# Lightning attention into a gated feed-forward layer: 64-token sub-blocks with two heads stacked on partitions, two sequences at once, crossbar transposes from block 8

## Chip, cores and metric

One core of one Trainium2 chip. Times are device microseconds (us) of one execution. A time is the median of a kernel's runs. Engine names are those of the profile: PE is TensorE's matmuls and PEld its weight loads, DVE is VectorE, ACT is ScalarE, POOL is GpSimd, SP is the sequencer that issues most DMAs here, and "SPq" and "POOLq" are the queues in which DMAs are issued.

## The reference, cut

```python
# q, k, v: (4, 8, 768, 64) float32;  lam: (8,);  w_in: (512, 2048);  w_out: (2048, 512)
for b in range(nb):                         # blocks of 64 tokens
    intra = (qb @ kb^T) * Dmask             # Dmask = lam ** (i - j) where i >= j, else 0
    out   = intra @ vb + (qb * lam_pow) @ kv_state
    kv_state = lam ** 64 * kv_state + (kb * rev_pow)^T @ vb
x = out as (3072, 512)                      # tokens x (heads * head_dim)
h = x @ w_in
out = (h * cos(h)) @ w_out                  # (3072, 512)
```

The feed-forward part is the larger one by far: 704 matmuls of 512 columns and 128 of 256 on PE. Attention feeds it.

## The kernel before: the parts that the change touches

A tile is 128 tokens of one sequence with all 8 heads, and there are 24 of them. The decay is split: q is scaled by a power of lam, v by its inverse. So the mask is of zeros and ones. A planner in the kernel simulates the engines and so fixes the order of instructions on every engine. What it decides is static program order: an instruction whose data is late holds up everything behind it on its engine.

```python
TILES = [4, 2, 4, 4, 4, 4, 2]                       # tiles per feed-forward group
ORDER = "b0 b1 b2 b3 i0 i1 i2 i3 o0 o1 o2 o3"       # first loads: tiles and weight chunks
...
# loads: one DMA of 256 KB per tensor and tile, 128 partitions (tokens)
i = nc.sync.dma_start(out=t, in_=src[b, :, s0:s0 + P, :].transpose([1, 0, 2]))
...
# transposes of q and k on PE, 8 matmuls of 128 columns per tile, then a DVE copy out of PSUM
nc.tensor.transpose(live["t", n][:, i, p, :], src[:, 2 * p:2 * p + 2, :], ident)
...
# q made block-diagonal (two heads per 128 partitions) by two DVE copies
nc.vector.tensor_copy(q_bd[n % NQ][h, :, i, :], t[h, 0, :, :])
...
# scores: 4 matmuls of 256 columns per tile
nc.tensor.matmul(t[:, 2 * i:2 * i + 2, :], lhsT=live["qkT", n][:, 1, p, :],
                 rhs=q_bd[n % NQ][:, p, :, :], start=True, stop=True)
...
# values: state and two heads, 12 matmuls of 128 columns per tile
nc.tensor.matmul(t[:, p, :], lhsT=kv_bd[(n - 1) % NK][:, p, :], rhs=live["qkT", n][:, 0, p, :], ...)
for i in range(2):
    nc.tensor.matmul(t[:, p, :], lhsT=v_pad[n % NV][:, 2 * p + i, :], rhs=live["s_m", n][:, 2 * p + i, :], ...)
```

## Time and profile before

| of the kernel before | value | view |
|---|---|---|
| time | 235.73 us (235.50 to 235.96, 2 runs) | run times |
| span | 233.6 us | the page |
| PE busy | 220.6 us, 94% | the page |
| first feed-forward matmul | 24.90 us | PE in order of time |
| DMA rate from 45 to 70 us | 228 GB/s | busy time by stretches |

The page is read from the top: busy time tells which engine is nearly full (PE), the rows of 40 slices tell when (a digit is the busy share of 5.84 us in tenths), and the chain of waits tells whether the full engine is also what sets the end. The lines are in the prediction below. One view that it does not show is that of PE's waits. Each line names the waiting engine and what ended the wait, then the us in total, how often, and the longest. In the kernel before no wait of PE on scores was longer than 1.1 us, and none of them was for a DMA:

```profile
PE ps_s L296 <- DVE qkT L271: 1.8, 3, 1.1
```

### The profile page before, as it was taken

How to read it: one execution, taken by the hardware profiler on the slowest of the kernel's cores; microseconds unless marked ns; L12 is line 12 of the kernel's file. 1: busy time of each engine (PE TensorE's matmuls, PEld its weight loads, DVE VectorE, ACT ScalarE, POOL GpSimd, SP SyncE). 2: the span in 40 equal slices, each digit the busy share in tenths (PEclk: the TensorE clock that was granted, in tenths of full speed). 3: DMA queues.
4: the chain of work that ended last, by engine and by line, in shares of the span. 5: the costliest groups of instructions: out<-in, count | busy, mean ns of one | idle time of the engine just before them, and what ended most of it. 6: DMA issues, size and time to landing. Idle time of an engine off the chain costs nothing.

```text
span 233.6 us, 4414 instructions
## 1 busy us (share of the span) xinstructions
PE 220.6 (94%) x1698; PEld 131.2 (56%) x1698; DVE 148.3 (63%) x279; ACT 106.6 (46%) x179; POOL 71.7 (31%) x108
## 2 busy tenths in 40 slices
PE   4887998899999999999999999999999999999993
PEld 4777543457776655555555555555555454556541
DVE  5577487087999998986685585685674563423210
ACT  5453676123445464554444445345345435544420
POOL 2569200486758665333314314412000000000000
PEclk9999999999999999999999999999999999999999
DMA  6997999999999999999562110110011011111112
GB/s 123 222 198 120 208 191 203 225 219 217 254 222 248 222 219 225 243 218 201 137 158 68 48 45 1 48 46 8 37 48 45 0 48 45 45 45 48 45 45 90
DMA packets 82868, 29.64 MB, mean 127 GB/s; under 512 B 75552, under 2 KB 79904, under 8 KB 82848
## 3 DMA queue, kind: packets, MB, share of 16 engines
q1 hardware_dynamic: 78480, 25.05, 48.6%
q0 software_dynamic: 4224, 4.19, 11.0%
q8 instruction: 13, 0.21, 0.4%
q10 hardware_dynamic: 144, 0.13, 0.2%
q14 instruction: 7, 0.06, 0.1%
HBM read 27.27 MB, written 6.29 MB: 144 GB/s over the span
## 4 chain that ended last, share of the span: by engine, by line
PE 71%; DVE 11%; DMA 10%; POOL 3%; ACT 2%; issue 1%; POOLq 0%
PE ps_f L410 30%; PE ps_h L372 26%; DMA w_out_sb<-in_moe_w_out_dram 8%; PE ps_s L296 4%; PE ps_t L266 4%; PE ps_o L341 4%; DVE q_bd L277 3%; DVE g L385 3%; DVE s_m L303 2%; DVE qkT L271 2%; PE ps_o L338 1%; PE ps_kv L316 1%; DMA lam_bc<-in_lam_dram 1%; POOL w_in_sb L214 1%; DVE kv_bd L325 1%; POOL w_out_sb L217 1%
## 5 line engine op out<-in xcount | busy, mean ns | idle before, releaser
L379 ACT ACTIVATE cos<-ps_h,halfpi 128x512 f32<-128x512 f32 (+1 forms) x107 | 66.3, 624 | 73.5 <-PE ps_h L372 73.4
L385 DVE TENSOR_TENSOR g<-ps_h,cos 128x512 bf16<-128x512 f32 (+1 forms) x107 | 64.5, 609 | 49.2 <-ACT cos L379 48.0
L410 PE MATMUL ps_f<-w_out_sb,g 128*128 128x512 bf16 x368 | 92.8, 379 | 1.4 <-ACT o_sb L423 0.7
L372 PE MATMUL ps_h<-xT,w_in_sb 128*128 128x512 bf16 (+1 forms) x428 | 93.7, 347 | 0.1
L372 PEld LDWEIGHTS <-w_in_sb 128*128 128x128 bf16 x448 | 43.0, 98 | 36.0 <-issue 0.4
L410 PEld LDWEIGHTS <-g 128*128 128x128 bf16 x384 | 35.9, 98 | 34.4 <-issue 2.2
L250 POOL TENSOR_TENSOR v_pad<-v_f,v_scale 128x256 bf16<-128x256 f32 x48 | 29.1, 626 | 46.7 <-PE ps_o L341 30.1
L303 DVE TENSOR_TENSOR s_m<-ps_s,mask 128x512 bf16<-128x512 f32 x48 | 31.3, 684 | 4.2 <-PE ps_s L296 4.1
L235 POOL TENSOR_TENSOR q_s<-q_f,q_scale 128x512 bf16<-128x512 f32 x23 | 24.0, 1043 | 22.5 <-PE ps_f L410 18.7
L271 DVE COPY qkT<-ps_t 128x1024 bf16<-128x1024 bf16 (+1 forms) x28 | 17.2, 614 | 17.3 <-PE ps_t L266 16.9
L423 ACT COPY o_sb<-ps_f 128x512 f32<-128x512 f32 x23 | 13.5, 586 | 21.7 <-PE ps_f L410 21.7
L277 DVE COPY q_bd<-qkT 64x512 bf16<-64x512 bf16 x48 | 19.6, 409 | 0.7
L341 PE MATMUL ps_o<-s_m,v_pad 128*128 128x128 bf16 x192 | 19.7, 221 | 0.4 <-DVE s_m L303 0.4
L350 ACT CAST xT<-ps_o 128x512 bf16<-128x512 f32 x24 | 14.0, 585 | 13.1 <-PE ps_o L341 13.0
L296 PE MATMUL ps_s<-q_bd,qkT 128*128 128x256 bf16 x96 | 15.6, 279 | 2.7 <-DVE qkT L271 1.8
L244 POOL CAST k_b<-k_f 128x512 bf16<-128x512 f32 x20 | 12.4, 620 | 17.6 <-issue 13.3
L341 PEld LDWEIGHTS <-v_pad 128*128 128x128 bf16 x192 | 14.9, 99 | 3.5 <-issue 0.5
L338 PE MATMUL ps_o<-qkT,kv_bd 128*128 128x128 bf16 x80 | 15.3, 219 | 0.0
L296 PEld LDWEIGHTS <-qkT 128*128 128x128 bf16 x96 | 8.8, 99 | 9.7 <-DVE q_bd L277 2.2
L325 DVE CAST kv_bd<-ps_kv 64x256 bf16<-64x256 f32 x32 | 13.4, 418 | 1.2 <-PE ps_kv L316 1.0
L468 PE MATMUL ps_h<-ident 128*128 128x64 bf16 x226 | 12.1, 211 | 1.6 <-POOL ident masks.py:199 1.6
L468 PEld LDWEIGHTS <-ident 128*128 128x128 bf16 x226 | 10.8, 111 | 1.8 <-POOL ident masks.py:199 1.6
(39 smaller groups left out, 93.1 us busy)
## 6 DMA issues: line engine op xcount, KB each, us to landing
q_f<-in_q_dram SPq DMA_DIRECT2D x24, 256.0 KB, 4.8
k_f<-in_k_dram SPq DMA_DIRECT2D x24, 256.0 KB, 4.8
v_f<-in_v_dram SPq DMA_DIRECT2D x24, 256.0 KB, 4.9
out_dram<-o_sb SPq DMA_DIRECT2D x23, 256.0 KB, 2.0
w_in_sb<-in_moe_w_in_dram POOLq DMA_DIRECT2D x4, 512.0 KB, 8.4
w_out_sb<-in_moe_w_out_dram POOLq DMA_DIRECT2D x4, 512.0 KB, 15.5
out_dram<-o_sb SPq DMA_DIRECT2D x1, 128.0 KB, 1.7
out_dram<-o_sb ACTq DMA_DIRECT2D x1, 128.0 KB, 1.7
```

Of the source, the lines that this page charges most:

```text
L235: eng.tensor_mul(t, live.pop(("q_f", n)), q_scale[:, c, :].unsqueeze(2).to_broadcast([P, H, D]))
L250: nc.gpsimd.tensor_mul(v_pad[n % NV][:, i::2, i * D:(i + 1) * D], src[:, i::2, :], v_scale[:, c, i::2].unsqueeze(2).to_broadcast([P, NP, D]))
L271: nc.vector.tensor_copy(live["qkT", n][:, sides], live["t", n][:, sides])
L277: nc.vector.tensor_copy(q_bd[n % NQ][h, :, i, :], t[h, 0, :, :])
L296: nc.tensor.matmul(t[:, 2 * i:2 * i + 2, :], lhsT=live["qkT", n][:, 1, p, :], rhs=q_bd[n % NQ][:, p, :, :], start=True, stop=True)
L303: nc.vector.tensor_mul(live["s_m", n][:, 4 * half:4 * half + 4, :], live.pop(("s", n, half)), mask.unsqueeze(1).to_broadcast([P, 4, P]))
L341: nc.tensor.matmul(t[:, p, :], lhsT=v_pad[n % NV][:, 2 * p + i, :], rhs=live["s_m", n][:, 2 * p + i, :], start=(i == 0 and c == 0), stop=( ...
L372: ins = nc.tensor.matmul(t[:, :cols], lhsT=w_in_sb[:, kd, f * P:(f + 1) * P], rhs=live["xT", i][:, kd, :cols], start=(kd == 0), stop=(kd = ...
L379: nc.scalar.activation(c[:, :cols], live["h", i, f][:, :cols], AF.Sin, bias=halfpi)
L385: nc.vector.tensor_mul(live["g", i][:, f, :cols], live.pop(("h", i, f))[:, :cols], live.pop(("c", i, f))[:, :cols])
L410: nc.tensor.matmul(live["f", i, j], lhsT=live["g", i][:, f, j * P:(j + 1) * P], rhs=w_out_sb[:, f, :], start=(f == 0), stop=(f == KF - 1))
L468: nc.tensor.matmul(idle_ps[:, :cols], lhsT=ident, rhs=ident[:, :cols], start=True, stop=True)
```

## The change

The intent is less work on PE. Blocks of 64 tokens halve the score and value columns, because less work above the diagonal is done. Two heads are stacked on the partitions: token t of head 0 on partitions 0 to 63, of head 1 on 64 to 127. So k and v (instead of q) are made block-diagonal. Two sequences are treated at once, as a pair of tiles; there are 12 pairs. From pair 4 (block 8) on, q and k are transposed by the DMA crossbar instead of PE. The diff, cut to its core:

```diff
-ORDER = "b0 b1 b2 b3 i0 i1 i2 i3 o0 o1 o2 o3"
+ORDER = "b0 b1 i0 i1 i2 i3 o0 o1 o2 o3"
+DMA_FROM = 4
...
-    for t in v_pad + q_bd + kv_bd:
-        nc.vector.memset(t, 0.0)
+    for a, b in zip(k_bd, v_bd):
+        nc.vector.memset(a, 0.0)
+        nc.gpsimd.memset(b, 0.0)
+    for a in kv_bd:
+        nc.gpsimd.memset(a, 0.0)
...
-                i = nc.sync.dma_start(out=t, in_=src[b, :, s0:s0 + P, :].transpose([1, 0, 2]))
+            x = x[b:b + 2, :, c * P + s * D:c * P + (s + 1) * D, :].rearrange("b (p i) s d -> i s (b p) d", i=2)
+            for h, i in halves:                       # partitions 0 to 63, then 64 to 127
+                ins = start(live[name, m][h, s], x[i])
...
+        def prep_vb(s):                               # v block-diagonal, on DVE
+            for h, i in halves:
+                nc.vector.tensor_copy(vb[h, s, :, :, h], live["v_c", m][h, s])
...
+        def transposes_dma(name, s):
+            nc.sync.dma_start_transpose(out=live[name, m][:, s].rearrange("t b p m -> t (b p) m"), in_=src)
...
+            if m >= DMA_FROM:
+                o, t = dma("SP", 1.2, 1.3, partial(transposes_dma, name, s), 2 * m - 6 + 0.1 * s + (name == "kT"),
+                           [ready], get=get, ordered=False)
...
-                    nc.tensor.matmul(t[:, 2 * i:2 * i + 2, :], lhsT=live["qkT", n][:, 1, p, :],
-                                     rhs=q_bd[n % NQ][:, p, :, :], start=True, stop=True)
+                    nc.tensor.matmul(t[:, s, p, :], lhsT=live["kT", m][:, s, x, p, :],
+                                     rhs=live["qT", m][:, 0, x, p, s * D:(s + 1) * D], start=True, stop=True)
```

## The prediction

> **What bounds the kernel now.** I read the page first: busy times, the slices and the chain of work that ended last.
>
> ```profile
> PE 220.6 (94%) x1698; PEld 131.2 (56%) x1698; DVE 148.3 (63%) x279; ACT 106.6 (46%) x179; POOL 71.7 (31%) x108
> ...
> PE   4887998899999999999999999999999999999993
> ...
> DMA  6997999999999999999562110110011011111112
> GB/s 123 222 198 120 208 191 203 225 219 217 254 222 248 222 219 225 243 218 201 137 158 68 48 45 1 48 46 8 37 48 45 0 48 45 45 45 48 45 45 90
> ...
> PE 71%; DVE 11%; DMA 10%; POOL 3%; ACT 2%; issue 1%; POOLq 0%
> ```
>
> PE (TensorE) is full from about 25 us to the end and carries 71% of the chain. The DMA row is as full as it gets, at 190 to 254 GB/s, from the start to about 105 us, and nearly empty after that. A slice is 5.84 us. So there are two regimes: a first half in which both PE and DMA are full, and a second half that is PE alone.
>
> Because a busy PE is not a PE at its peak, I next took the instructions in order of time, which give the rate of each kind of matmul once it runs back to back:
>
> ```profile
> 24.07 0.89 PE L468 MATMUL ps_h<-ident 128*128 128x64 bf16 x25
> 24.90 1.89 PE L372 MATMUL ps_h<-xT,w_in_sb 128*128 128x512 bf16 x8
> ...
> 51.00 0.39 PE L266 MATMUL ps_t<-ident,k_b 128*128 128x128 bf16 x4
> ...
> 62.37 0.60 PE L372 MATMUL ps_h<-xT,w_in_sb 128*128 128x256 bf16 x4
> ...
> 226.93 2.75 PE L410 MATMUL ps_s<-w_out_sb,g 128*128 128x512 bf16 x12
> ```
>
> The spans include some 0.2 us of pipeline depth (one lone matmul of 128 columns takes 0.22 us). Taken off, a 128-column matmul costs 56 ns, a 512-column one 216 ns, a 256-column one 109 ns, and a 64-column one 29 ns, its own weight load included. All are columns / 2400 + 2.5 ns. With these rates I counted PE's own instruction order from the first feed-forward matmul (24.90 us) on: 704 of 512 columns (152.0 us), 128 of 256 (14.0), and for the attention of the last 20 tiles 452 of 128 and 80 of 256 columns (33.9 us). Sum 199.9 us. The last matmul ends at 229.7, that is 204.8 us after the first, so only 4.9 us are lost in the whole steady part. A tail of 3.9 us follows (evacuation, store, end). The median of the times is 2.1 us above the profiled span.
>
> Last, the DMA queue's issues:
>
> ```profile
> 39.80 0.37 SPq L199 DMA_DIRECT2D q_f<-in_q_dram  x1
> ...
> 47.84 1.08 SPq L199 DMA_DIRECT2D v_f<-in_v_dram  x1
> 49.01 1.09 SPq L199 DMA_DIRECT2D q_f<-in_q_dram  x1
> ...
> 117.35 0.37 SPq L199 DMA_DIRECT2D q_f<-in_q_dram  x1
> ```
>
> An issue takes 0.37 us when the queue is free and about 1.08 us when it is full: 256 KB per 1.1 us is the transfer rate itself, so SP (the issuing sequencer) is held back by the transfers. The loads of tile 4 start only at 39.8 us, after the third w_out chunk has landed. From there to 105 us every load goes out as fast as the DMA engines take it.
>
> **What the Trainium skill says.** "TensorE: Matmul & The Clock Gate", Back-to-back issue gap: warm, N / 2.4 + 2.5 ns, with a floor of about 25 ns up to 64 columns; the trace agrees (29 ns at 64, 56 at 128, 216 at 512). "DMA: Bandwidth & Descriptors", Queues, rings and completion order: each engine takes descriptors in ring order; the trace agrees as far as the steady 4.8 us to landing behind a full queue goes. The same page, Latency and other measured facts, gives a crossbar transpose 261 GB/s; no run yet shows it, and I estimate 256 KB at 1.0 to 1.2 us. The same page, Rules for kernel authors, says transfers to the two partition halves serialize: the split k and v loads will not be faster than whole ones.
>
> **The change part by part, on PE.** Per tile before: 8 transposes (0.45), 4 score matmuls of 256 columns (0.44), 4 updates (0.22), 12 values (0.67), together 1.78 us. After, per pair of tiles: 16 scores, 16 updates, 32 values, all of 64 columns: 64 x 29.2 ns = 1.87 us, so 0.93 us per tile. Blocks of 64 tokens halve the score and value columns, because above-diagonal work is no longer done. Transposes are 24 per pair (k is block-diagonal, thus twice as many): 1.34 us per pair for pairs 0 to 3, and none on PE from pair 4. Counted in the changed instruction order from the first feed-forward matmul: 152.0 + 14.0 unchanged, 616 of 64 columns (18.0), 48 transposes (2.7): 186.6 us. The gain on PE is 199.9 - 186.6 = 13.3 us, 5.6% of the time.
>
> The other engines. DVE (VectorE) loses q_bd (two of 0.41 us per tile), one transpose evacuation of 0.69 per tile from pair 4 and half of the state copies, and gains the v_bd copies (four of 0.41 per pair): some 3.7 us per tile become 2.2. It was 98% busy from 60 to 80 us, so this stage gets easier. POOL: per pair 2.1 (q) + 2.5 (k in four pieces) + 2.1 (v) = 6.7 us against 2 x 2.9 = 5.8 before, well under the 15.5 us that PE needs per pair. ACT gains two state copies of 0.37 to 0.6 per pair, off the path. At the start POOL gets six memsets and both q products; the start is bound by loads of the same size, so I leave it at 24.9 us, give or take 2.
>
> If the 4.9 us of losses and the tail stay, the sum is 24.9 + 186.6 + 4.9 + 3.9 = 220.3 of span, 222.4 us of time.
>
> **What the transposes do to the DMA queue.** From pair 4 on, 3 transposes of 256 KB per pair join the queue that is full until 105 us. In SP's instruction order those of pair 4 stand behind all loads of pairs 5 and 6, and those of pair 5 behind the loads of pair 7 (its k behind q of pair 8 too). SP cannot run ahead of the transfers, as the 1.08 us issues show. So what has to pass from the first load of pair 2 (about 39 us) until pair 5 has its k transposed is: 6.33 pairs of 1.57 MB = 9.96 MB, 4 stores (1.05 MB) and 6 transposes (1.57 MB), 12.6 MB. At 235 GB/s that is 53.5 us, so 92.5 us; at 254, the best slice, 88.5; at 225, 95. PE, in order, stands at pair 4's scores after 41.1 us of work, near 24.9 + 41.1 + 2 = 68 us, where the data (9.4 MB, about 40 us) come near 79; and at pair 5's scores after 6.8 us more. PE has 138.7 us of work left after pair 5's scores (308 + 248 of 512 columns, 64 of 256, 400 of 64). So 92.5 + 138.7 + 3.9 = 235.1 of span, 237.2 us of time (233 to 240 for the rates above). From pair 6 on the queue catches up: 14.8 us of PE work before its scores, 9 us of transfers.
>
> **The rivals.** (a) The gain arrives: 222 us. For it: PE is full from 80 us to the end, and the prefetch depth shrinks from four tiles to three pairs but is deeper in bytes. Against it: the queue order above. It needs the transposes to reach the data sooner than the order says, or loads faster than 254 GB/s. (b) The transposes arrive late and PE waits about 11 us at pair 4 and some 6 at pair 5: 237 us, all gain gone. For it: the full DMA row up to 105 us and SP's 1.08 us issues. Against it: the writer of the change chose block 8 as the start of the transposes, presumably with a reason, so my reading of the queue may be too strict. (c) A 64-column matmul with fresh weights costs more than 29 ns, say 40: 616 x 11 ns = 7 us back, 229 us without stalls. For it: the 29 ns were measured with one and the same weights (ident). Against it: each of those had its own weight load, and 128-column ones with fresh weights keep 56 ns. (d) The split loads, 64 partitions each, run below 217 GB/s; then (b) grows by 4 to 6 us, to 242.
>
> **Range and chances.** I give (b) in some form 55% and (a) with part of (c) 45%: 0.55 x 237 + 0.45 x 223 = 231 us. This is a mean of two cases more than a peak. The range that should hold 8 in 10 is 220 to 241. Faster by over 2% means under 231.0: 0.47. Slower by over 2% means over 240.4: 0.14. Within 2%: 0.39.
>
> **What would show it right or wrong.** PE's step: attention groups of 64 columns should run at 29 ns, so that 8 take about 0.41 us with depth; the total from first feed-forward matmul to last should be 186.6 us plus stalls. The stall: the waits should name PE ps_s (scores) or its weight load waiting on DMA kT or qT, once near 68 to 79 us and once near 86 to 93, and the slices between should show PE at 3 to 6 tenths with DMA full. If PE has no gap there, (b) is wrong and the time is near 222. SP: transposes at 1.0 to 1.2 us in the queue; if each takes several us, everything in (b) shifts later and the time is over 241. The start: if the first feed-forward matmul is far from 24.9 us, POOL's memsets are the first suspect. DVE should show about 110 us busy and no waits near 60 to 80 us.

## The result and the profile after

The changed kernel takes 256.75 us (256.42 to 257.08, 2 runs) against 235.73 us, and its results are right. The ratio is 1.089, with a 95% interval of 1.082 to 1.097: slower, and outside the range. A ratio here is the mean time of one kernel's fast runs over that of the other's of the same rounds, so it is not quite the ratio of the medians.

The page of the kernel after: busy time, then the slices (now 6.36 us each) of PE, of its granted clock, of the DMA engines and their rate, then the chain.

```profile
PE 216.4 (85%) x1971; PEld 124.2 (49%) x1971; DVE 132.5 (52%) x223; ACT 120.2 (47%) x201; POOL 87.3 (34%) x102
...
PE   7197899879863095599959999999999999999994
...
PEclk9779999999999659799988999999999999999999
DMA  6999999997879989999996999809111110112112
GB/s 122 186 190 192 198 200 212 211 205 169 215 160 220 212 184 190 201 196 196 208 169 165 162 216 243 123 32 137 41 44 43 41 41 3 41 41 83 45 41 82
...
PE 59%; SPq 11%; DVE 10%; DMA 8%; POOL 6%; issue 3%; ACT 2%; POOLq 0%
```

PE was full from 25 us on before. Now it has holes: between 70 and 108 us the row falls to 6, 3, 0 and 5 tenths, and it drops to 5 once more at about 130 us. The DMA row is full until about 160 us instead of 105, and it is full at mostly 160 to 220 GB/s where it had been at 190 to 254. PE's share of the chain fell from 71 to 59%, and the SP queue came in with 11%.

PE in order of time names the holes. The columns are start, length, engine, line, operation and tiles; the bracket tells how long the engine had stood idle and what ended it.

```profile
78.06 1.03 PE L476 MATMUL ps_f<-w_out_sb,g 128*128 128x512 bf16 x4
87.88 0.39 PE L351 MATMUL ps_s<-qT,kT 128*128 128x64 bf16 x4 [8.80 <-DMA kT<-k_bd]
...
103.88 0.29 PE L351 MATMUL ps_s<-qT,kT 128*128 128x64 bf16 x4 [3.70 <-DMA kT<-k_bd]
...
105.29 1.90 PE L476 MATMUL ps_f<-w_out_sb,g 128*128 128x512 bf16 x4
...
131.00 0.29 PE L351 MATMUL ps_s<-qT,kT 128*128 128x64 bf16 x4 [1.90 <-DMA kT<-k_bd]
132.26 0.82 PE L351 MATMUL ps_s<-qT,kT 128*128 128x64 bf16 x12 [0.97 <-DMA kT<-k_bd]
```

These are the scores of pairs 4, 5 and 7, each waiting for the crossbar transposes of k. Two more things are to be seen. The third wait, at pair 7, was not foreseen at all. And the four matmuls of 512 columns at 105.29 us, right after a hole, take 1.90 us, while the same four at 78.06 us took 1.03: from 105 to 108 us, after the hole, PE was granted half its clock (0.50). The Trainium skill has this in "TensorE: Matmul & The Clock Gate", Part 1: The HAM clock gate, which gives half clock after an idle window of about 3.4 us and a return after about as long of sustained work. The trace agrees in kind. After the 8.80 us hole, score and value matmuls of 64 columns stand 53 ns apart instead of 29 until about 94 us, some 5 us.

The SP queue in order of time shows why k comes late:

```profile
74.09 0.57 SPq L221 DMA_DIRECT2D q_f<-in_q_dram  x1
74.75 2.20 SPq L494 DMA_DIRECT2D out_dram<-o_sb  x1
77.08 2.66 SPq L221 DMA_DIRECT2D k_f<-in_k_dram  x4
80.26 2.64 SPq L221 DMA_DIRECT2D v_f<-in_v_dram  x4
83.07 1.33 SPq L329 DMA_TRANSPOSE qT<-q_s  x1
84.53 2.65 SPq L329 DMA_TRANSPOSE kT<-k_bd  x2
...
98.41 4.32 SPq L329 DMA_TRANSPOSE kT<-k_bd  x2
...
124.45 5.84 SPq L329 DMA_TRANSPOSE kT<-k_bd  x2
```

The transposes of pair 4 (83.07 and 84.53 us) stand behind all loads of pair 6 (74.09 to 82.90 us). This is the order that the prediction had read from the program. The two at 98.41 us are those of pair 5, the two at 124.45 us those of pair 7. Every load of k and v is now four transfers of 128 KB, and four take about 2.65 us, 0.66 us each: 198 GB/s.

How the two rates compare over one stretch in which only loads and a few stores run, 45 to 70 us, first before, then after (the last two numbers of a line are the DMA engines' share and the GB/s):

```profile
45.00:70.00 25.00, 24.14 (x232) 17.21 (x230) 20.58 (x42) 8.43 (x17) 17.29 (x25) 1.00 1.13 228
```

```profile
45.00:70.00 25.00, 22.18 (x236) 13.42 (x235) 17.00 (x25) 7.36 (x14) 18.70 (x21) 1.00 0.93 200
```

At the start, the first feed-forward matmul came at 29.50 us instead of 24.90. POOL zeroed v_bd and kv_bd until 10.5 us, and only then scaled the first q (start, length, then the operation):

```profile
2.52 5.31 POOL L154 MEMSET v_bd<- 128x2048 bf16 x3
7.78 2.75 POOL L156 MEMSET kv_bd<- 128x1024 bf16 x3
10.61 1.90 POOL L278 TENSOR_TENSOR q_s<-q_f,q_scale 128x1024 bf16<-128x1024 f32 x1
```

### The profile page after: what moved, and what is told of

It is laid out like the page before. It is cut to its first block, busy times and chain, and to the rows that moved or that the text cites. A ratio compares the mean times of both kernels' runs of the same rounds, so it can differ in the third digit from the quotient of the medians.

```text
span 254.4 us, 4988 instructions
## 1 busy us (share of the span) xinstructions
PE 216.4 (85%) x1971; PEld 124.2 (49%) x1971; DVE 132.5 (52%) x223; ACT 120.2 (47%) x201; POOL 87.3 (34%) x102
## 4 chain that ended last, share of the span: by engine, by line
PE 59%; SPq 11%; DVE 10%; DMA 8%; POOL 6%; issue 3%; ACT 2%; POOLq 0%
PE ps_f L476 26%; PE ps_h L438 23%; SPq L221 8%; DMA v_f<-in_v_dram 5%; DVE v_bd L295 5%; SPq L329 3%; POOL v_c L290 2%; PE ps_t L317 2%; PE ps_f L438 2%; POOL v_bd L154 2%; PE ps_o L385 2%; DVE kT L323 1%; PE ps_o L383 1%; DMA kT<-k_bd 1%; PE ps_s L351 1%
## 5 line engine op out<-in xcount | busy, mean ns | idle before, releaser
L278 POOL TENSOR_TENSOR q_s<-q_f,q_scale 128x1024 bf16<-128x1024 f32 x12 | 22.8, 1901 | 53.5 <-DMA q_f<-in_q_dram 38.9
L357 DVE TENSOR_TENSOR s_m<-ps_s,mask 128x512 bf16<-128x512 f32 x24 | 16.1, 687 | 22.5 <-PE ps_s L351 22.4
L290 POOL TENSOR_TENSOR v_c<-v_f,v_scale 128x512 bf16<-128x512 f32 x24 | 24.7, 1040 | 8.6 <-DMA v_f<-in_v_dram 7.7
L285 POOL CAST k_bd<-k_f 64x512 bf16<-64x512 f32 x40 | 24.5, 613 | 4.8 <-DMA k_f<-in_k_dram 2.8
L295 DVE COPY v_bd<-v_c 64x512 bf16<-64x512 bf16 x48 | 24.2, 505 | 0.5
L351 PE MATMUL ps_s<-qT,kT 128*128 128x64 bf16 x192 | 10.2, 203 | 16.8 <-DMA kT<-k_bd 16.7
L374 ACT CAST kv_bd<-ps_kv 64x512 bf16<-64x512 f32 x26 | 15.1, 580 | 12.7 <-PE ps_kv L370 8.5
L385 PE MATMUL ps_o<-s_m,v_bd 128*128 128x64 bf16 x192 | 16.0, 197 | 1.4 <-DVE s_m L357 1.4
L383 PE MATMUL ps_o<-qT,kv_bd 128*128 128x64 bf16 x176 | 15.7, 197 | 0.2 <-ACT xT L391 0.2
L385 PEld LDWEIGHTS <-v_bd 128*128 128x128 bf16 x192 | 13.2, 101 | 4.7 <-issue 1.5
L383 PEld LDWEIGHTS <-kv_bd 128*128 128x128 bf16 x176 | 13.4, 101 | 3.2 <-issue 0.6
```

The lines of the kernel that those rows point to most:

```text
L278: nc.gpsimd.tensor_mul(t, live.pop(("q_f", m)).rearrange("t (b h) d -> t b h d", b=2), q_scale[:, c, :].unsqueeze(1).unsqueeze(3).to_broad ...
L285: (nc.scalar.copy if early else nc.gpsimd.tensor_copy)(kb[h, s, :, :, h], src[h])
L290: nc.gpsimd.tensor_mul(live["v_c", m][:, s], live["v_f", m][:, s].rearrange("t (b p) d -> t b p d", b=2), v_scale[:, 2 * c + s, :].unsquee ...
L295: nc.vector.tensor_copy(vb[h, s, :, :, h], live["v_c", m][h, s])
L351: nc.tensor.matmul(t[:, s, p, :], lhsT=live["kT", m][:, s, x, p, :], rhs=live["qT", m][:, 0, x, p, s * D:(s + 1) * D], start=True, stop=True)
L374: (nc.scalar.copy if eng == "ACT" else nc.vector.tensor_copy)(kv_bd[(2 * m + s) % NK][h, :, :, h], kv_ps[h])
```

## The experiments

Two theories stood after this reading, and the expectations go by them. One is the order: the transposes stand behind prefetch loads in the SP queue. (The expectations call this theory A.) The other is the rate: the loads of k and v over 64 partitions each are slower than those over 128, so that everything in the queue is late, the transposes among it (B; later B1, if the number of transfers does it, and B2, if the 64 partitions do). A third suspect was the late start (D). Each experiment starts from the changed kernel unless it says otherwise.

### pe_all: no crossbar transposes at all

```diff
-DMA_FROM = 4
+DMA_FROM = 12
-            dv[s] = pl.add("POOL", 1.05, [load_t["v_f", m, s], table], ...
+            dv[s] = pl.add("POOL", 1.05, [load_t["v_f", m, s], table] + ([dv[0]] if s else []), ...
```

The second edit only keeps the two halves of v in order, since the first of them allocates their buffer.

> All transposes on TensorE, no crossbar transposes anywhere; everything else as in the changed kernel. Theory A (the transposes of pair 4 on stand in the load queue behind prefetches, and PE waits for them): the three gaps of PE between 75 and 135 us vanish, at a price of 8 x 1.34 = 10.7 us of matmul time. First feed-forward matmul stays near 29 us, so 29 + 197.3 + about 5 + 3.9 = 235 us of span, 237 us of time, some 19 us faster than the changed kernel. Rival B (the split 64-partition loads are too slow to feed PE, whoever transposes): PE still has gaps over 5 us in all between 60 and 110 us and the time stays over 243 us.

Measured: results right, 241.32 us in the fast run (245.72 in the slow; before 235.58). The span is 239.6 us, and PE waits for no transpose. So without any crossbar transposes the changed kernel is still some 6 us slower than the one before, but 15 us faster than with them. The PE count of the prediction, plus 8 pairs x 1.34 us of transposes, plus the late start (30.22 us for the first feed-forward matmul), gives 30.2 + 186.6 + 10.7 + 4.9 + 3.9 = 236.3 of span. The measured 239.6 is 3.3 us above that, which slower loads may account for. PE was busy for 47.3 of the 50 us from 60 to 110 us, so rival B, with gaps of over 5 us there, is out. What follows: where they stand, the crossbar transposes cost more than they save. What the slower loads cost without them is not shown; by this count, which lets the 4.9 us of losses stay, it is about 3 us.

### whole: k and v loaded over 128 partitions

```diff
-            for h, i in halves:
-                ins = start(live[name, m][h, s], x[i])
-            return ins
+            return start(live[name, m][:, s], x[b + s, :, c * P:(c + 1) * P, :].rearrange("h t d -> t h d"))
```

The same bytes go in half as many transfers of 256 KB. The rows land in the wrong places, so the results are wrong.

> Wrong numbers on purpose: k and v are loaded with 128 partitions per transfer, 256 KB each (one batch per transfer), instead of two transfers of 64 partitions and 128 KB; same bytes, same buffers, same readers. Theory B (split loads slow the queue: 0.6 us of issue per 128 KB, 197 GB/s instead of 228 between 39 and 75 us): the rate between 39 and 75 us returns to about 225 GB/s, the scores of pair 4 come near 80 instead of 88 us, and the time drops by 8 us or more, below 249 us. If the split is harmless: rate and time stay within 2 us of 256.7.

Measured: 245.19 us, ratio 1.040. The rate from 45 to 70 us is back:

```profile
45.00:70.00 25.00, 23.31 (x269) 14.78 (x268) 17.40 (x30) 9.41 (x18) 21.14 (x25) 1.00 1.09 230
```

and the two waits come where the prediction had put them (79 and 92.5 us, or 95 at 225 GB/s):

```profile
80.57 0.40 PE L348 MATMUL ps_s<-qT,kT 128*128 128x64 bf16 x4 [5.36 <-DMA kT<-k_bd]
...
96.09 0.29 PE L348 MATMUL ps_s<-qT,kT 128*128 128x64 bf16 x4 [3.63 <-DMA kT<-k_bd]
```

What follows: with loads near the old rate (223 GB/s from 39 to 96 us, transposes included) the arithmetic of the queue holds. The rate is worth 11.6 us. It is not the whole loss.

### order: loads behind the transposes of two pairs earlier

```diff
+    for m in range(DMA_FROM + 2, NBLK // 2):
+        issue_t["q_f", m].deps += [t.issue for t in (Tq[m - 2, 0], Tk[m - 2, 0], Tk[m - 2, 1])]
```

> Same transfers and same work; only SP's instruction order changes: the loads of pair m are issued after the transposes of pair m - 2 (from pair 6 on), so that a transpose has one pair of loads ahead of it instead of two. Theory A: the scores of pair 4 come near 76 us instead of 88, those of pair 5 near 85 instead of 104, and the time drops by 15 to 25 us, to 232 to 242 us. If the amount of DMA work and not its order sets the time (rival C): PE's gaps move but their sum stays, and the time stays above 250 us.

Measured: results right, 244.32 us (243.0 to 245.65), ratio 1.037. Pair 4's scores come at 79.31 and pair 5's at 92.33 us, each with some 2 us of wait instead of 9.6 and 4.3. PE's waits on transposes fell from 16.7 us to:

```profile
PE ps_s L351 <- DMA kT<-k_bd: 4.9, 5, 1.2
```

What follows: the order in the queue is worth 12.4 us, about as much as the rate. (The two runs lie 2.65 us apart, so this is good to some 1.3 us.) One reading in passing: the four 512-column matmuls at 94.25 us took 1.90 us here too, half clock, though none of the waits before them (2.60, 1.20 and 0.89 us) was as long as 3.4 us. The granted clock in narrow stretches shows that it fell after the first of them: it was full until 89.8 us and 0.50 from 90.2 us on, before the two shorter waits, and the eight matmuls after the wait of 2.60 us took 2.35 us instead of 1.89:

```profile
88.79 2.35 PE L438 MATMUL ps_h<-xT,w_in_sb 128*128 128x512 bf16 x8 [2.60 <-DVE g L451]
```

### start: POOL's zeroing in 4-byte words

```diff
-        nc.gpsimd.memset(b, 0.0)
+        nc.gpsimd.memset(b.bitcast(mybir.dt.uint32), 0)
-        nc.gpsimd.memset(a, 0.0)
+        nc.gpsimd.memset(a.bitcast(mybir.dt.uint32), 0)
```

> Only the six memsets on POOL are written as 4-byte words, half the elements. Theory D (POOL's 8.1 us of memsets make the first attention late): POOL is free some 4 us earlier and the first feed-forward matmul comes 2 to 4 us earlier than at 29 us. If the loads behind the weights set the time later on, as theory A says, the end moves by less than 1.5 us; if the start is on the path of the end, it moves by the full 2 to 4 us.

Measured: results right, 258.04 us (257.47 to 258.62), ratio 1.095. The zeroing takes half as long and the first feed-forward matmul comes at 26.89 instead of 29.50 us, but the end does not come earlier. The first load of pair 2 starts at 40.47 instead of 39.08 us, since it waits for weight chunks and not for POOL.

```profile
2.51 2.75 POOL L154 MEMSET v_bd<- 128x1024 uint32 x3
5.21 1.47 POOL L156 MEMSET kv_bd<- 128x512 uint32 x3
```

What follows: the late start is real (4.6 us) but not on the path that sets the end. That path leads through the DMA queue: PE's longest wait for a transpose grew from 8.8 to 12.7 us.

### small128: as many transfers as in the change, over 128 partitions

```diff
-            x = x[b:b + 2, :, c * P + s * D:c * P + (s + 1) * D, :].rearrange("b (p i) s d -> i s (b p) d", i=2)
-            for h, i in halves:
-                ins = start(live[name, m][h, s], x[i])
+            for i in range(2):
+                ins = start(live[name, m][:, s, i * NP:(i + 1) * NP],
+                            x[b + s, i * NP:(i + 1) * NP, c * P:(c + 1) * P, :].rearrange("h t d -> t h d"))
```

Results are wrong, as in whole.

> Wrong numbers on purpose: k and v come in eight transfers of 128 KB per pair, as in the changed kernel, but each over all 128 partitions (4 rows of 256 B per partition) instead of 64. If the number of transfers and their issue cost slows the queue (theory B1): about 200 GB/s from 39 to 75 us and a time near 256, as the changed kernel. If writing to only 64 partitions does it (theory B2): about 228 GB/s and a time near 245, as the run with 256 KB transfers over 128 partitions.

Measured: 246.38 us, ratio 1.046. The rate is 217 GB/s from 45 to 70 us (224 from 39 to 75), and pair 4's and 5's scores come at 81.88 and 96.67 us, so this is whole and not the change:

```profile
81.88 0.39 PE L351 MATMUL ps_s<-qT,kT 128*128 128x64 bf16 x4 [5.74 <-DMA kT<-k_bd]
```

The issues of k in the queue (least, median and longest ns, first and last start), in the changed kernel and here:

```profile
L221 SPq DMA_DIRECT2D k_f<-in_k_dram x48: 601/634/3758, 1.7 to 147.0; - x48
```

```profile
L221 SPq DMA_DIRECT2D k_f<-in_k_dram x48: 368/522/2876, 1.7 to 137.6; - x48
```

What follows: neither the size of 128 KB nor the number of transfers makes the loads slow. Their shape does: 64 partitions of 8 runs (which also means 64 tokens, 16 KB, in a row in memory) against 128 partitions of 4 runs. An issue over 64 partitions takes 0.60 us at the least, one over 128 takes 0.37.

### order_whole: both causes taken away

The edits of order and of whole together; results wrong.

> Wrong numbers on purpose: whole 128-partition loads and the transposes ahead of the prefetches together. If these two are the cause of the waits (-11.5 and -12.4 us alone), PE's gaps between 75 and 135 us nearly vanish: 29 + 186.6 + 6 + 3.9 = 225.5 us of span; if they add only partly, up to 236 us of time. Above 240 us a third cause is as large.

Measured: 235.15 us, ratio 0.998 (0.992 to 1.004). Against the changed kernel these are 21.6 us, where the two alone had given 12.4 and 11.6. PE's waits on transposes are nearly gone:

```profile
PE ps_s L348 <- DMA kT<-k_bd: 1.6, 2, 1.1
```

What follows: the two causes nearly add up (21.6 us of 24.0) and together are as large as the loss against the kernel before. Taking them away does not bring the gain of 13.3 us that PE's count promised: the first feed-forward matmul comes 5.5 us later (30.4 instead of 24.9), and PE loses 7.2 us more than the kernel before in waits afterwards, the largest of them on gating products (3.1 us) and on copies of the state (2.4 us). That a mended start would now shorten the time was not tried.

### f8nm: what can be kept and gives right results

Crossbar transposes only from pair 8 (`DMA_FROM = 8`), the edits of order and start, and the kept order of v's halves.

> Correct version meant to be fast: crossbar transposes only from pair 8, when the load queue has emptied, and ahead of the loads of pair m + 2; memsets in 4-byte words. Against the version with all transposes on TensorE (243.5 us) PE saves 4 x 1.34 = 5.4 us and the start up to 2.6 us: theory A expects 235 to 239 us and no wait of PE on a transpose over 1 us. If crossbar transposes hurt in themselves (rival E, they slow loads or PE wherever they run): 243 us or more.

Measured: results right, 239.20 us (238.48 to 239.93), ratio 1.015 (1.007 to 1.023). PE waits for no transpose, and the first feed-forward matmul comes at 25.74 us. But POOL waits for the loads, and PE for POOL:

```profile
POOL q_s L278 <- DMA q_f<-in_q_dram: 40.0, 9, 19.4
...
PE ps_kv L370 <- POOL v_c L290: 3.6, 2, 2.3
```

What follows: with the order mended and the start too, the slow loads remain (205 GB/s from 45 to 70 us), and the best right version of this form was still 1.5% slower than the kernel before. The time lies just above the 235 to 239 us expected; the expectation had also started from 243.5 us, a median with a slow run in it, where the fast run of pe_all took 241.32. Rival E is out. The load queue had not emptied by pair 8, as the expectation has it: loads and transposes went on side by side (198 GB/s from 100 to 140 us), and with the transposes ahead of the loads none was late.

### pool_half: the upper halves of k and v from a second queue

From pair 2 on, the transfer to partitions 64 to 127 is issued from POOL's queue, so that both halves are in flight at once. The kept order of v's halves is in as well.

```diff
-                ins = start(live[name, m][h, s], x[i])
+                if part is None or part == i:
+                    ins = start(live[name, m][h, s], x[i], nc.gpsimd if part == 1 else nc.sync)
```

> Correct. As the changed kernel (transposes from pair 4, in the old order), but from pair 2 on the upper partition half of k and v is loaded from POOL's queue and the lower half from SP's, so that both partition halves are written at the same time. Theory B2 (only half of the partitions is written at a time, and that limits the rate): 220 GB/s or more from 45 to 70 us instead of 200, the scores of pair 4 near 80 us instead of 88, and a time of 244 to 250 us. If the limit is a cost per 64-partition transfer on whatever queue: 200 GB/s and 255 us or more, POOL's issues (about 0.8 us each) coming on top.

Measured: results right, 261.68 us, ratio 1.110. The rate does not rise, and the transfers take longer to land (KB each, then us from issue to landing; in the changed kernel it was 3.8 us for k):

```profile
45.00:70.00 25.00, 22.94 (x203) 13.76 (x202) 10.57 (x21) 8.09 (x16) 17.99 (x23) 1.00 1.12 192
```

```profile
k_f<-in_k_dram POOLq DMA_DIRECT2D x20, 128.0 KB, 6.4
```

What follows: either it is not the writing of one half at a time that makes the loads slow, or a second queue does not mend it. The DMA engines were busier than in the changed kernel (share 1.12 against 0.93) at a lower rate, so it was not for want of issued transfers. But the test is not a clean one: POOL's DMAs go by another kind of queue, and POOL's own work waits while it issues.

### f8pool: the same on top of f8nm

With the casts of k for pairs 2 to 5 on ACT, to free POOL.

> Correct version meant to be fast: transposes from pair 8 and ahead of the prefetches, memsets in 4-byte words, the two halves on two queues, k of pairs 2 to 5 cast on ACT to make room on POOL. The version without the two queues took 239.2 us, PE losing some 13 us between 40 and 90 us. Theory B2: at 225 GB/s half of that goes, 231 to 236 us, at or below the kernel before (235.7). Rival: POOL's issues delay its own casts, and the time stays at 239 us or more.

Measured: results right, 249.14 us (247.52 to 250.25, 4 runs), ratio 1.059 (1.055 to 1.063). The rate is 199 GB/s. It is 10 us slower than f8nm: the second queue gives nothing here either. How much of the 10 us is its cost is not shown, since the casts were moved to ACT in the same run, and PE waited 2.7 us for one of them.

A load of k in one transfer that covers both halves in the right places is said to have failed to build, because its access pattern has more than three dimensions. So what in the 64-partition transfers is slow (the number of partitions or the rows in memory) stays open.

### xb12 and xb10: the kernel before with crossbar transposes for late tiles

These start from the kernel before. Tiles 12 (or 10) to 23 get their q and k transposed by the crossbar, with loads over 128 partitions as they were, and with the transposes of tile n ahead of the loads of tile n+3.

```diff
+XBAR_FROM = 12
...
+        def by_dma():
+            o, tq = dma("SP", 0.6, 0.7, lambda: transposes_dma(0), n - 6, [a], get="qkT", ordered=False)
+            o2, To[n] = dma("SP", 0.6, 0.7, lambda: transposes_dma(1), n - 5.9, [b, o], ordered=False)
...
+        first_out, q_there = (by_dma if n >= XBAR_FROM else by_engine)()
...
+    for n in range(XBAR_FROM + 3, NBLK):
+        issue_t["q_f", n].deps += x_issue[n - 3]
```

> The kernel before in its 128-token form, unchanged but for tiles 12 to 23: their q and k are transposed by two DMA transposes instead of eight TensorE matmuls and one PSUM copy, and these DMAs stand on the SP queue ahead of the loads of the tile three further. Results must be right. Theory (the loss of the changed kernel came from transposes behind loads and from 64-partition loads, not from the DMA transposes as such): 12 tiles lose 8 matmuls of 56 ns each, 5.4 us of TensorE, so about 230.3 us, if no TensorE wait on a transpose is longer than 1 us. Rival (the load stream is still running up to about 105 us, any transpose joined to the queue arrives late and its wait eats what it saves): 235 us or more, with waits of TensorE on the transposed tile in the trace.

> The same with tiles 10 to 23 by DMA: 14 tiles save 14 x 8 x 56 ns = 6.3 us, so about 229.4 us under the theory; under the rival the two further tiles, which fall earlier in the load stream, make it slower than the run from tile 12.

Measured: both right; xb12 235.95 us, ratio 1.001 (0.996 to 1.006); xb10 239.76 us, ratio 1.018 (1.013 to 1.023). PE's busy time in xb12 fell by 6.2 us to 214.4 (some matmul records are missing from the trace; by count it is 5.4), but the span only by 0.8. DVE, then PE, in order of time:

```profile
90.69 0.96 DVE L279 COPY q_bd<-qkT 64x512 bf16<-64x512 bf16 x2 [2.55 <-DMA qkT<-q_s]
```

```profile
93.33 1.67 PE L392 MATMUL ps_h<-xT,w_in_sb 128*128 128x512 bf16 x7 [2.81 <-DVE g L405]
```

PE did not wait for the transposed tile itself. DVE did, and behind that copy in DVE's order stood the gating products (g) that free the PSUM banks of the feed-forward matmuls. In xb10 these waits of DVE were seven instead of two:

```profile
DVE q_bd L279 <- DMA qkT<-q_s: 11.2, 7, 3.4
```

What follows: the rival was right about the time and about late transposes. Its sign, PE waiting for the transposed tile, did not come: the saving on PE is lost by way of an engine that is not the bottleneck.

### xb14: the same from tile 14, with the waiting copies later in DVE's order

```diff
-XBAR_FROM = 12
+XBAR_FROM = 14
-            T[n] = To[n]
+            T[n] = To[n]; tq.lat = To[n].lat = 5.0
```

The second line tells the planner that a transpose lands 5 us after its issue; it moves one pair of q_bd copies behind two gating products and a mask product on DVE and changes nothing in PE's order.

> As the run from tile 12, with tiles 14 to 23 by DMA and with the copies that wait for the first transposed tile a little later in VectorE's order. The run from tile 12 took 6.2 us off TensorE's busy time and won only 0.8 us of span: VectorE stood 0.8 and 2.5 us for the transposes of tiles 12 and 13, with the gating products of the FFN behind it, and TensorE stood 2.8 us for those. Theory (those two waits were what the rest was lost to, and tiles 14 on cost nothing): 10 tiles x 8 x 56 ns = 4.5 us, about 231.2 us, and no wait of VectorE on a transposed tile over 0.5 us. Rival (the first tiles that go by DMA always wait, since the load stream runs on and is slowed by the transposes): waits of 1 to 3 us at tile 14 or 15 in the place of those at 12 and 13, and 233.5 us or more.

Measured: results right, 233.18 us (fast runs 232.51 to 233.37; one run of 236.71 was slow), against 235.72 in the same rounds. The ratio is 0.987 (0.983 to 0.991), so this is 1.3% faster than the kernel before, clear of noise, and the fastest version. The time lies between the theory's 231.2 and the rival's 233.5. The wait came as the rival had it (1 to 3 us, where the theory allowed 0.5), but only once, at the first tile that goes by the crossbar:

```profile
DVE q_bd L279 <- DMA qkT<-q_s: 1.7, 1, 1.7
...
PE ps_h L392 <- DVE g L405: 1.4, 1, 1.4
```

(The two lines are of DVE's and of PE's waits.) Half of the 4.5 us of transposes taken from PE arrive at the end: the span is 231.4 instead of 233.6 us. The load stream had not ended: the transposes began at 90.0 us, and loads were issued between them until 136 us. Two things were changed against xb12, the first tile and the place of the copies, and no run tells what each is worth.

## Why the prediction was wrong, point by point

- **PE's work: right.** From 136 to 250 us of the changed kernel PE has no hole. The 799 matmuls that start in that stretch are, by the prediction's rates, 113.9 us of work in 114.0 us, and matmuls of 64 columns with fresh weights stand 29 ns apart at full clock. Rival (c), a dearer 64-column matmul, is out.
- **The mechanism of rival (b): right.** The transposes of pairs 4 and 5 stood behind prefetch loads, and PE waited at both places (and at pair 7, see below). The weight of 45% on (a) was misplaced: what spoke for it (PE full from 80 us on, deeper prefetch, and that whoever chose block 8 must have had a reason) did not answer the order in the queue. The number 231 was a mean of two cases, so it was right in neither.
- **The size of (b): the step that failed.** "At 235 GB/s that is 53.5 us, so 92.5 us" took the rate of loads over 128 partitions for loads over 64. Measured from 39 to 75 us, the rate was 196 GB/s (228 in the kernel before). At that rate the same 12.6 MB take 64.3 us, from 39.1 to 103.4 us (the trace has 199 GB/s over that stretch); pair 5's scores came at 103.88, 11.4 us after 92.5. These are 11.4 of the 19.3 us by which the span (254.4) exceeds the 235.1 of (b). In run whole pair 5's scores came at 96.09 us: so 7.8 of the 11.4 us are shown to be the 64-partition loads, and the other 3.6 fit 235 being too high even for loads over 128 partitions with transposes among them (223 GB/s). The rate alone would not have saved the prediction: whole still took 245.19 us, 8 more than the 237.2 of (b), because of these 3.6 us and for the reasons in the next two points. Rival (d) named this cause, but allowed it 4 to 6 us. The prediction had cited the rule that two partition halves serialize, and read from it that split loads are not faster, when the question was by how much they are slower.
- **"From pair 6 on the queue catches up": wrong.** Pair 7 waited 2.9 us more (1.90 and 0.97), and again for the order in the queue: POOL had its q and k ready by 97.6 us, but its transposes stood behind the loads of pair 9, those of k behind q of pair 10 too. From the last transpose of pair 6 to the last of pair 7 SP was issuing for 16.2 us (114.1 to 130.3), 3.1 MB at about 194 GB/s, an estimate from the sizes, while PE had 8.9 us of work between their scores (120.23 to 129.10).
- **Half clock after a hole: left out.** After pair 5's wait the slowed matmuls cost about 1.7 us (two groups of four 512-column matmuls, 0.87 and 0.62, and the scores, 0.2), after pair 7's about 1.5. After pair 4's it cost nothing, because pair 5 was waiting for its transposes anyway. With 0.55 us of second wait at pair 5 these make 11.4 + 2.9 + 3.2 + 0.6 = 18.1 of the 19.3 us. The last 1.2 us are not attributed.
- **The start: outside its margin, without effect.** 29.50 us instead of 24.9 give or take 2, by POOL's zeroing, as suspected. Run start took 2.6 us of it off and the end did not come earlier.
- **"If the 4.9 us of losses stay": wrong.** Even with both causes taken away (order_whole) PE lost 233.0 - 30.4 - 186.6 - 3.9 = 12.1 us to small waits. A likely reading, not tested, is that with less work PE reaches more often what POOL, DVE and ACT have not finished.
- **DVE: about 110 us predicted, 132.5 measured.** The v_bd copies took 505 ns in the mean instead of 410; the rest of the excess was not followed up, since DVE is half idle. POOL's 6.7 us per pair were right (1.90 + 4 x 0.61 + 2 x 1.04 = 6.4), and so, nearly, was the time of a transpose in the queue (1.30 us for k and 1.33 for q in the median, up to 4.49 behind a full queue, against 1.0 to 1.2).

## What to carry to other kernels

Before work is moved from a full engine to the DMA queues, look at the DMA row in the stretch concerned: where it is full, a transfer that the bottleneck needs at once can wait behind all that was prefetched, and here the saving came back as holes, with half clock after three of them. Split a load by partitions only after its rate has been measured, and read program order on engines beside the bottleneck too, since one early copy that waits for a DMA holds up everything behind it. Here the crossbar paid only in the old form of the kernel, from tile 14 on, with each transpose ahead of the later loads in the queue; loads still ran beside them, and only the first of these tiles was waited for.

## What the Trainium skill lacked or had wrong

- "DMA: Bandwidth & Descriptors", Rules for kernel authors, says that transfers to two partition halves serialize, from one queue or from two; run pool_half agrees (192 GB/s with two queues). That row gives no rate. With k and v in loads of 128 KB over 64 partitions the queue moved 196 to 200 GB/s, the shortest issue taking 0.60 us; with loads of 128 KB over 128 partitions it moved 217 to 224 GB/s, the shortest taking 0.37 us. This is no gap of the skill as a whole: another of its pages treats loads over 64 partitions.
- The same page, Latency and other measured facts, gives a rate for the crossbar transpose, 261 GB/s, and no time in the queue. A transpose of 256 KB took at least 1.25 us of the SP queue (about 210 GB/s, an estimate from the two), one of 128 KB at least 1.19 us, so nearly the same. To landing it was 4.0 us for k and 4.2 for q in the median with the queue full of loads in the changed kernel, and 2.4 us at the least in the run from tile 12.
- "TensorE: Matmul & The Clock Gate", Part 1, gives half clock after an idle window of about 3.4 us. Shorter gaps were followed by it here: in run order one of 2.60 us (the clock fell at about 90.1 us, 1.3 us after its end, and four matmuls of 512 columns took 1.90 instead of 1.03 us), in run f8nm one of 2.32 us (0.50 from 86.0 us). In run xb12 a gap of 2.81 us was followed by full clock, so the length of a gap alone does not tell.
- "VectorE: DVE Perf Modes", Zero memsets can be issued as uint32, speaks of VectorE alone. It holds for POOL as well: zeroing 128 x 2048 elements of 2 bytes took 1.8 us each, and 0.9 us as 4-byte words (5.31 and 2.75 us for three).
